# Attention's first scores ahead of the next pair's transposes, five more warm products, the first k on ScalarE's queue, and mask products in bf16 behind the others

## Chip, cores and metric

One Trainium2 chip, one core. The metric is the time of one execution in device microseconds (us). The kernel before was timed in three runs: 858.63, 860.8 and 864.05 us, a median of 860.8 us. One more execution was profiled; its rows are the ones read here.

## The reference

Three layers follow one another: block-causal attention, a mixture of experts that picks one expert per token, and a two-layer network with a leaky activation. The change touches the first alone.

```python
def _attn_ref(q, k, v):                      # q, k, v: (4, 8, 576, 64)
    scores = scale * np.matmul(q, k.transpose(0, 1, 3, 2))
    mask = block_i >= block_j                # blocks of 64 positions
    scores = np.where(mask, scores, -1000000000.0)
    scores = scores - np.max(scores, axis=-1, keepdims=True)
    attn = np.exp(scores)
    attn = attn / (np.sum(attn, axis=-1, keepdims=True) + 1e-09)
    return np.matmul(attn, v)

def reference(**kw):
    x = attn_out.transpose(0, 2, 1, 3).reshape(2304, 512)
    x = _moe_ref(x, ...)                     # gate, argmax over 8 experts, relu(x w1) w2
    return _moe2_ref(x, ...)                 # (leaky(x w_in)) w_out
```

## The kernel before

Attention runs over 16 pairs of heads (4 batches, 4 pairs each). For a pair `p`, `load` (line 186) brings q, k and v with three transfers each, all issued by SyncE's queue (SP). `tr` (line 198) transposes four 128x128 tiles of q (`psq`) or k (`psk`) on TensorE (PE); `split_qk` (line 210) has ScalarE (ACT) write the high part (`qh`, `kh`) and VectorE (DVE) the rest (`ql`, `kl`). `tr_tail` (line 218) does the same for the last 64 positions (`pst`), whose q goes into two block-diagonal tiles of `qd`.

`sc(p, i)` (line 228) makes the scores of one block of rows, in the order i = 4, 3, 2, 1, 0. For i < 4 it has n = 128 i + 128 columns of keys. Each of the three products of `PARTS` (`qh·kh`, `qh·kl`, `ql·kh`, line 236) is issued as two instructions, one for each head, on 64 rows of the array each. Between the first and the second product stands the mask product (line 239): `top` by `neg` adds -2^30 to the last 64 columns of the rows that may not see them. For i = 4 the block-diagonal `qd` needs no mask (line 243). A score block lies in one of two PSUM buffers (`ps_s`). Then `row_max` (DVE, lines 250 and 253), `expo` (ACT, lines 267 and 270), `ptr` (transposes of the exponentials on PE, lines 286 to 301, copied by ACT or DVE, lines 275 and 277), `pv` (products with v, lines 314 and 326) and `xout` (lines 350 to 358).

A table of offsets `OFF` (line 513) gives each step of each pair its place, so that the steps of neighbouring pairs interleave; a scheduler then orders the instructions of each engine by priority and its own estimates. What stands on an engine runs strictly in that order. At the start `warm` (line 57) issues eight bf16 products of 512 columns without use (`psw`), behind the first `load`, while the first transfers are under way.

After attention the tokens are routed, lists are scattered to memory and read back, and the experts run, fed by large weight loads of which two are under way at a time (`bulk`, line 78); the last layer follows.

Of the kernel before, what the change touches and what calls it, by code (L numbers as in the profile page):

```python
# [9 lines left out]
F32 = mybir.dt.float32  # L10
F32R = mybir.dt.float32r
BF16 = mybir.dt.bfloat16
I32 = mybir.dt.int32
AF = mybir.ActivationFunctionType
ALU = mybir.AluOpType
AX = mybir.AxisListType
# [3 lines left out]
B, H, S, D = 4, 8, 576, 64  # L20
# [17 lines left out]
WARM = 8  # L38
NEG = -float(2 ** 30)
# [8 lines left out]
def tile_kernel(ctx: ExitStack, tc: tile.TileContext, q, k, v, w_skip, w_gate, w1, w2, w_in, w_out, alpha, out):  # L48
    nc = tc.nc
    dram = lambda n, s, dt: nc.dram_tensor(n, s, dt, kind="Internal").ap()  # L50
    xd = dram("xd", (NT + 1, DM), F32)
    def free(ins, group):
        ins = ins.ins
        tc.declare_no_dep(ins, group=group, reason="rows of one token each")
        tc.add_to_no_dep_group(group, ins)

    def warm(pool, tag, n):
        if n == 0:
            return
        ps = pool.tile([128, 2, 4, 128], F32, tag=tag, name="psw")  # L60
        for i in range(n):
            nc.tensor.matmul(ps[:, 0], ones, ones.unsqueeze(1).to_broadcast([128, 4, 128]), start=True, stop=True)

    def apart():
        nc.gpsimd.memset(pad, 0)
# [54 lines left out]
    acst = actx.enter_context(tc.tile_pool(name="acst", bufs=1))  # L120
    ident = const.tile([128, 128], F32, name="ident")
# [5 lines left out]
    ones = const.tile([128, 128], BF16, name="ones")  # L127
# [16 lines left out]
    nc.vector.memset(fill, PADROW)  # L144
    tlo = acst.tile([128, 5], I32, name="tlo")
    nc.vector.tensor_scalar(out=tlo, in0=tok, scalar1=63, scalar2=None, op0=ALU.bitwise_and)
    top = acst.tile([128, 128], F32R, name="top")
    nc.vector.memset(top.bitcast(F32), 0.0)
    for r in (0, 64):
        nc.vector.memset(top[r:r + 1, 0:64].bitcast(F32), 1.0)  # L150
    neg = acst.tile([128, 64], F32R, name="neg")
    nc.vector.memset(neg.bitcast(F32), NEG)
    thi = acst.tile([128, 5], F32, name="thi")
    nc.vector.tensor_tensor(out=thi, in0=tok, in1=tlo, op=ALU.subtract)
    sli = const.tile([128, 2, 2], F32, name="sli")
# [23 lines left out]
    st = [dict() for _ in range(NPAIR)]  # L179
# [4 lines left out]
    half = [slice(0, 64), slice(64, 128)]  # L184

    def load(p, nm, src):
        b, h0 = p // NP, p % NP * 2
        a = ld.tile([128, 5, 2, D], F32, tag=nm + "r", name=nm + "r")
        for x in range(2):
            nc.sync.dma_start(out=a[:, 0:4, x, :], in_=src[b, h0 + x, 0:512, :].rearrange("(t p) d -> p t d", p=128))  # L190
        nc.sync.dma_start(out=a[0:64, 4], in_=src[b, h0:h0 + 2, 512:S, :].rearrange("h p d -> p h d"))
        st[p][nm + "r"] = a

    def tok4(p, nm, t):
        n = 128 if t < 4 else 64
        return st[p][nm + "r"][0:n, t].rearrange("p h d -> p (h d)")

    def tr(p, nm):
        ps = ps_m.tile([128, 512], F32, tag="m", name="ps" + nm)
        for t in range(4):  # L200
            nc.tensor.transpose(ps[:, t * 128:t * 128 + 128], tok4(p, nm, t), ident)
        for c in "hl":
            st[p][nm + c] = tp.tile([128, 512 if nm == "q" else S], F32R, tag=nm + c, name=nm + c)
        split_qk(nm, *(st[p][nm + c][:, 0:512] for c in "hl"), ps)
# [5 lines left out]
    def split_qk(nm, hi, lo, ps):  # L210
        scale = 0.125 if nm == "q" else 1.0
        nc.scalar.activation(out=hi, in_=ps, func=AF.Copy, scale=scale)
        if nm == "q":
            nc.vector.scalar_tensor_tensor(out=lo, in0=ps, scalar=scale, in1=hi.bitcast(F32), op0=ALU.mult, op1=ALU.subtract)
        else:
            nc.vector.tensor_tensor(out=lo, in0=ps, in1=hi.bitcast(F32), op=ALU.subtract)

    def tr_tail(p):
        ps = ps_m.tile([128, 2, 64], F32, tag="m", name="pst")
        for n, nm in enumerate("qk"):  # L220
            nc.tensor.transpose(ps[:, n, :], tok4(p, nm, 4), ident[0:64, 0:64])
        for x, hs in enumerate(half):
            split_qk("q", *(qd[p % 2][hs, c, x * 64:x * 64 + 64] for c in range(2)), ps[hs, 0, :])
        split_qk("k", *(st[p]["k" + c][:, 512:S] for c in "hl"), ps[:, 1, :])
# [3 lines left out]
    def sc(p, i):  # L228
        d = st[p]
        ps = d["s", i] = ps_s.tile([128, 2, 512], F32, tag="s", name="pss")  # L230
        if i < 4:
            n = 128 * i + 128
            qc = slice(i * 128, i * 128 + 128)
            for k, (a, b) in enumerate(PARTS):
                for x, hs in enumerate(half):
                    nc.tensor.matmul(ps[:, x, 0:n], d[a][hs, qc], d[b][hs, 0:n], start=(k == 0), stop=(k == 2))  # L236
                if k == 0:
                    for x, hs in enumerate(half):
                        nc.tensor.matmul(ps[:, x, n - 64:n], top[hs], neg[hs], start=False, stop=False)
        else:  # L240
            for c, o in ((slice(0, 512), ps[:, 0]), (slice(512, S), ps[:, 1, 0:64])):
                for k, (a, b) in enumerate(PARTS):
                    nc.tensor.matmul(o, qd[p % 2][:, int(a == "ql")], d[b][:, c], start=(k == 0), stop=(k == 2))

    def row_max(p, i):
        d = st[p]
        ps = d["s", i]
        if i < 4:
            m = sm.tile([128, 2], F32, tag="mx", name="mx", bufs=4)
            nc.vector.tensor_reduce(out=m, in_=ps[:, :, 0:128 * i + 128], axis=AX.X, op=ALU.max, negate=True)  # L250
        else:
            m = sm.tile([128, 1], F32, tag="m4", name="m4", bufs=2)
            nc.vector.tensor_reduce(out=m, in_=ps.rearrange("p x c -> p (x c)")[:, 0:S], axis=AX.X, op=ALU.max, negate=True)
        d["m", i] = m

    last_exp = [None]
# [262 lines left out]
    for p in range(NPAIR):  # L519
# [11 lines left out]
        if p % NP == NP - 1:  # L531
            b = p // NP
            last = p == NPAIR - 1
            n = NP - 1 if last else NP
# [25 lines left out]
    order = sorted(events)  # L560
    cut = 5 * NPAIR + OFF["xo"]
    gaps = {route2: 8, route4: 4}
    start = {load: WARM}
    for s in order:
        if s < cut:
            for fn, a in events[s]:
                fn(*a)
                warm(ps_s, "s", start.pop(fn, 0))
# [4 lines left out]
    for s in order:  # L573
        if s >= cut:
            for fn, a in events[s]:
                if fn in gaps:
                    warm(ps_s, "s", gaps[fn])
                fn(*a)
# [5 lines left out]
    ps = ps_m.tile([128, E], F32, tag="m", name="psl")  # L584
# [6 lines left out]
    def scatter(o, ids):  # L591
        free(nc.gpsimd.indirect_dma_start(out=xd, out_offset=bass.IndirectOffsetOnAxis(ap=ids, axis=0), in_=o, in_offset=None, bounds_check=NT - 1, oob_is_err=False), "xd")

    warm(ps_s, "s", 13)
    xgs = [stat.tile([128, DM], F32, tag=f"xg{g}", name="xgs") for g in range(2)]
    gather(xgs[0], sid[:, 0:1])
# [424 lines left out]
    for n, (w, f) in enumerate(seq):  # L1021
        if n + 2 < len(seq):
            g1(*seq[n + 2])
        t = (f - 5) // 2
# [43 lines left out]
```

## Time and profile before

| | |
|---|---|
| timed runs, median (lowest, highest) | 860.8 us (858.63, 864.05) |
| the profiled execution, its time | 854.09 us |
| its span, first to last instruction | 852.5 us |
| PE busy, share of the span | 799.0 us, 94% |
| DVE, ACT, GpSimd (POOL) busy | 458.8, 299.3, 162.4 us |
| mean granted clock of PE | 0.97 of full speed |
| attention's score blocks | about 12 to 241 us |

The profiled execution is 6.7 us below the median of the timed runs. A share of busy time is a mean over stages with different limits; a matmul's duration in a row contains its way through the array, so what a product costs on PE is read from the distance between the starts of rows that follow one another. "PEld" rows are the loads of the stationary operand, which can run under a product. "[idle before <-releaser]" says how long the engine stood idle and who ended that.

### The profile page before, as it was taken

How to read it: one execution, taken by the hardware profiler on the slowest of the kernel's cores; microseconds unless marked ns; L12 is line 12 of the kernel's file. 1: busy time of each engine (PE TensorE's matmuls, PEld its weight loads, DVE VectorE, ACT ScalarE, POOL GpSimd, SP SyncE). 2: the span in 40 equal slices, each digit the busy share in tenths (PEclk: the TensorE clock that was granted, in tenths of full speed). 3: DMA queues.
4: the chain of work that ended last, by engine and by line, in shares of the span. 5: the costliest groups of instructions: out<-in, count | busy, mean ns of one | idle time of the engine just before them, and what ended most of it. 6: DMA issues, size and time to landing. Idle time of an engine off the chain costs nothing.

```text
span 852.5 us, 14562 instructions
## 1 busy us (share of the span) xinstructions
PE 799.0 (94%) x5548; PEld 613.9 (72%) x5548; DVE 458.8 (54%) x951; ACT 299.3 (35%) x779; POOL 162.4 (19%) x204
## 2 busy tenths in 40 slices
PE   7999999999986899998599988999999999999998
PEld 4777777777753665765388666888888888888887
DVE  4576757667657167798579898323222332222232
ACT  3777676766641123112143433211111112111111
POOL 1000110110103122313012211321222212222132
PEclk7999999999998799999799999999999999999999
DMA  6765354464313777877723221100110001000100
GB/s 123 169 197 143 87 147 108 96 159 126 95 36 89 251 254 244 267 254 240 239 101 94 80 83 42 50 0 1 50 50 0 1 26 50 0 1 1 38 13 25
DMA packets 96378, 85.84 MB, mean 101 GB/s; under 512 B 68601, under 2 KB 73913, under 8 KB 96272
## 3 DMA queue, kind: packets, MB, share of 16 engines
q1 hardware_dynamic: 93776, 78.88, 32.1%
q0 software_dynamic: 2496, 5.61, 2.0%
q8 instruction: 59, 0.97, 0.5%
q14 instruction: 47, 0.39, 0.2%
HBM read 73.20 MB, written 11.71 MB: 100 GB/s over the span
## 4 chain that ended last, share of the span: by engine, by line
PE 47%; DVE 9%; DMA 4%; issue 2%; ACT 1%; SPq 0%; DVEq 0%; ACTq 0%
PE psf L970 18%; PE psa L1001 6%; PE psa L1002 6%; PE psa L1011 6%; PE psh L752 4%; PE psy L763 3%; DVE dt L640 2%; DMA w2t<-in_moe_w_dram 1%; DVE dr L644 1%; DVE dt L641 1%; DVE gt L983 1%; DMA w1t<-in_moe_w_dram 1%; PE psh L777 1%; DVE dr L642 1%; DVE dr L638 1%
## 5 line engine op out<-in xcount | busy, mean ns | idle before, releaser
L970 PE MATMUL psf<-xs,whi 128*128 128x512 f32 (+1 forms) x640 | 159.6, 371 | 0.7 <-ACT xs L856 0.7
L987 POOL TENSOR_TENSOR gl<-gt,gh 128x512 fp32r<-128x512 f32 (+1 forms) x80 | 96.0, 1200 | 322.9 <-ACT gh L986 190.5
L986 ACT ACTIVATE gh<-gt 128x512 fp32r<-128x512 f32 (+1 forms) x80 | 47.1, 589 | 264.5 <-PE psa L1002 144.7
L970 PEld LDWEIGHTS psf<-xs,whi 128*128 128x128 f32 x640 | 114.3, 188 | 25.4 <-ACT xs L856 0.9
L982 DVE TENSOR_SCALAR gu<-psf,alf 128x512 f32<-128x512 f32 (+1 forms) x64 | 43.7, 683 | 158.3 <-PE psf L970 158.0
L970 PE MATMUL psf<-xs,wlo 128*128 128x512 f32 (+1 forms) x320 | 80.1, 372 | 0.0
L267 ACT ACTIVATE pe<-pss,mx 128x512 f32<-128x512 f32 (+3 forms) x128 | 66.6, 524 | 14.2 <-DVE mx L250 11.8
L970 PEld LDWEIGHTS psf<-xs,wlo 128*128 128x128 f32 x320 | 56.6, 188 | 11.7
L1001 PE MATMUL psa<-whi,gh 128*128 128x512 f32 x144 | 57.3, 398 | 6.5 <-ACT gh L986 6.5
L250 DVE TENSOR_REDUCE mx<-pss 128x2 f32<-128x1024 f32 (+1 forms) x64 | 52.4, 819 | 19.9 <-PE pss L236 17.3
L275 ACT ACTIVATE pt<-pspt 128x512 f32<-128x512 f32 (+3 forms) x112 | 52.1, 488 | 29.4 <-PE pspt L301 28.7
L1001 PE MATMUL psa<-wkg,gh 128*128 128x512 f32 x144 | 57.2, 397 | 1.7 <-ACT gh L986 1.7
L983 DVE SCALAR_TENSOR_TENSOR gt<-psf,gu 128x512 f32<-128x512 f32 (+1 forms) x80 | 51.0, 637 | 13.9 <-POOL gl L987 8.1
L1002 PE MATMUL psa<-wlo,gh 128*128 128x512 f32 x144 | 56.3, 391 | 0.0
L1002 PE MATMUL psa<-wkg,gh 128*128 128x512 f32 x144 | 56.3, 391 | 0.0
L301 PE MATMUL pspt<-ident,pe 128*128 128x128 f32 x320 | 51.5, 287 | 0.1
L326 PE MATMUL pso<-pt,vr 128*64 128x256 f32 (+1 forms) x384 | 47.5, 352 | 2.3 <-ACT pt L275 2.1
L857 DVE TENSOR_TENSOR xs<-psx,xs 128x512 fp32r<-128x512 f32 x18 | 12.4, 692 | 60.4 <-ACT xs L856 60.4
L326 PEld LDWEIGHTS pso<-pt,vr 128*64 128x64 f32 x384 | 30.1, 136 | 16.9 <-ACT pt L275 7.2
L752 PEld LDWEIGHTS psh<-xT,w1t 128*128 128x128 f32 x320 | 39.5, 205 | 1.5 <-issue 1.0
L752 PE MATMUL psh<-xT,w1t 128*128 128x128 f32 x320 | 40.2, 290 | 0.0
L301 PEld LDWEIGHTS pspt<-ident,pe 128*128 128x128 f32 x320 | 33.8, 141 | 6.7 <-issue 2.2
(231 smaller groups left out, 1374.3 us busy)
## 6 DMA issues: line engine op xcount, KB each, us to landing
w1t<-in_moe_w_dram SPq DMA_DIRECT2D x32, 512.0 KB, 4.5
w2t<-in_moe_w_dram SPq DMA_DIRECT2D x32, 512.0 KB, 4.5
dr<-in_moe_w_in_dram SPq DMA_DIRECT2D x16, 512.0 KB, 5.1
dr<-in_moe_w_out_dram SPq DMA_DIRECT2D x16, 512.0 KB, 3.7
out_dram<-ob SPq DMA_DIRECT2D x18, 256.0 KB, 2.0
qr<-in_q_dram SPq DMA_DIRECT2D x32, 128.0 KB, 4.9
kr<-in_k_dram SPq DMA_DIRECT2D x32, 128.0 KB, 2.6
vr<-in_v_dram SPq DMA_DIRECT2D x32, 128.0 KB, 2.5
```

What stands on the lines that cost most here:

```text
L250: nc.vector.tensor_reduce(out=m, in_=ps[:, :, 0:128 * i + 128], axis=AX.X, op=ALU.max, negate=True)
L267: ins = nc.scalar.activation(out=pt[:, x, 0:n], in_=ps[:, x, 0:n], func=AF.Exp, bias=m[:, x:x + 1], scale=1.0, accum_out=d["sum"][:, x * 4 ...
L275: nc.scalar.activation(out=o, in_=a, func=AF.Copy)
L301: nc.tensor.transpose(ps[:, y, j, :], e[:, x, j * 128:j * 128 + 128], ident)
L326: nc.tensor.matmul(d["o"][hs, c0:c0 + n * 128], v5[:, j, x, :], pt[:, x, 2 * j:2 * j + n].rearrange("p n c -> p (n c)"), start=(j == 0), s ...
L752: nc.tensor.matmul(ps[:, f], w[:, kk, c:c + 128], self.xT[:, kk], start=(kk == 0), stop=(kk == 3))
L970: nc.tensor.matmul(ps[:, 0:n], wsp[f // 4 * 4 + kk][a][:, ws], c[:, kk, 0:n], start=(n0 == 0 and kk == 0), stop=(n0 == 2 and kk == 3))
L983: nc.vector.scalar_tensor_tensor(out=t[:, 0:n], in0=ps[:, 0:n], scalar=0.0, in1=u[:, 0:n], op0=ALU.max, op1=ALU.add)
L987: nc.gpsimd.tensor_tensor(out=lo[:, 0:n], in0=t[:, 0:n], in1=hi[:, 0:n].bitcast(F32), op=ALU.subtract)
L1001: nc.tensor.matmul(o, hi[:, ts], whi, start=(f == 0), stop=False)
L1002: nc.tensor.matmul(o, hi[:, ts], wlo, start=False, stop=False)
L1011: nc.tensor.matmul(acc[w, t], lo[:, t * 128:t * 128 + 128], whi, start=False, stop=False)
```

## The change

It makes four edits. The first three act on the first pair, the fourth on every pair.

1. The first transpose of the second pair's q waits for the first row maximum (a dependency on DVE's reduce of `sc(0, 4)`), so that the first scores stand ahead of it.
2. `warm` issues five more products behind `tr_tail` of the first pair (the first of them is kept behind the tail transposes in the schedule).
3. The three transfers of the first pair's k are issued by ACT's queue instead of SP's.
4. `top` and `neg` are bf16 and not fp32r, and the mask product stands behind the third product of `PARTS` and closes the accumulation, which the third product did before.

```diff
     def warm(pool, tag, n):
...
         for i in range(n):
-            nc.tensor.matmul(ps[:, 0], ones, ones.unsqueeze(1).to_broadcast([128, 4, 128]), start=True, stop=True)
+            ins = nc.tensor.matmul(ps[:, 0], ones, ones.unsqueeze(1).to_broadcast([128, 4, 128]), start=True, stop=True)
+            if i == 0 and tail[0]:
+                tc.add_manual_dep(ins.ins, tail[0].name, mybir.DependencyInfo(mybir.DependencyClass.NoSync, mybir.DependencyReason.SCHED_ONLY), reason="behind the transposes")
...
-    top = acst.tile([128, 128], F32R, name="top")
-    nc.vector.memset(top.bitcast(F32), 0.0)
+    top = acst.tile([128, 128], BF16, name="top")
+    nc.vector.memset(top, 0.0)
...
-    neg = acst.tile([128, 64], F32R, name="neg")
-    nc.vector.memset(neg.bitcast(F32), NEG)
+    neg = acst.tile([128, 64], BF16, name="neg")
+    nc.vector.memset(neg, NEG)
...
     def load(p, nm, src):
+        queue = nc.scalar if p == 0 and nm == "k" else nc.sync
         for x in range(2):
-            nc.sync.dma_start(out=a[:, 0:4, x, :], in_=src[b, h0 + x, 0:512, :].rearrange("(t p) d -> p t d", p=128))
+            queue.dma_start(out=a[:, 0:4, x, :], in_=src[b, h0 + x, 0:512, :].rearrange("(t p) d -> p t d", p=128))
...
     def tr(p, nm):
         for t in range(4):
-            nc.tensor.transpose(ps[:, t * 128:t * 128 + 128], tok4(p, nm, t), ident)
+            ins = nc.tensor.transpose(ps[:, t * 128:t * 128 + 128], tok4(p, nm, t), ident)
+            if p == 1 and nm == "q" and t == 0:
+                tc.add_manual_dep(ins.ins, st[0]["first"].name, mybir.DependencyInfo(mybir.DependencyClass.Sync, mybir.DependencyReason.DATA), reason="first scores first")
...
             for k, (a, b) in enumerate(PARTS):
                 for x, hs in enumerate(half):
-                    nc.tensor.matmul(ps[:, x, 0:n], d[a][hs, qc], d[b][hs, 0:n], start=(k == 0), stop=(k == 2))
-                if k == 0:
-                    for x, hs in enumerate(half):
-                        nc.tensor.matmul(ps[:, x, n - 64:n], top[hs], neg[hs], start=False, stop=False)
+                    nc.tensor.matmul(ps[:, x, 0:n], d[a][hs, qc], d[b][hs, 0:n], start=(k == 0), stop=False)
+            for x, hs in enumerate(half):
+                nc.tensor.matmul(ps[:, x, n - 64:n], top[hs], neg[hs], start=False, stop=True)
...
-    start = {load: WARM}
+    start = {load: WARM, tr_tail: 5}
```

PE at the start, before: behind the first pair's transposes of k (`psk`) and of the tails (`pst`) stand the second pair's of q (`psq`), then the first scores (`pss`).

```order
L201 MATMUL psk<-ident,kr 128x128 x4
L221 MATMUL pst<-ident,qr 128x64
L221 MATMUL pst<-ident,kr 128x64
L201 MATMUL psq<-ident,qr 128x128 x4
L243 MATMUL pss<-kh,qd_168 128x512
L243 MATMUL pss<-kl,qd_168 128x512
L236 MATMUL pss<-kh,qh 128x512 x2
L243 MATMUL pss<-kh,qd_168 128x512
```

The same place after the change (the pair of rows with `ones` stands five times).

```order
L206 MATMUL psk<-ident,kr 128x128 x4
L228 MATMUL pst<-ident,qr 128x64
L228 MATMUL pst<-ident,kr 128x64
L64 LDWEIGHTS ones
L64 MATMUL psw<-ones 128x512
...
L249 MATMUL pss<-kh,qd_168 128x512
L249 MATMUL pss<-kl,qd_168 128x512
...
L243 MATMUL pss<-kh,qh 128x512 x2
L243 MATMUL pss<-kl,qh 128x512 x2
L243 MATMUL pss<-kh,ql 128x512 x2
...
L206 MATMUL psq<-ident,qr 128x128 x4
```

The second pair's four transposes moved from ahead of the first two score blocks to behind them, and the five products `psw` stand where they were.

ACT at the start, before: the two writes of `qd` that the first scores need stand on either side of the second pair's `qh`.

```order
L212 ACT_TABLE_LOAD
L212 ACTIVATE qh<-psq 128x512
L212 ACTIVATE kh<-psk 128x512
L212 ACTIVATE qd_168<-pst 64x64
L212 ACTIVATE qh<-psq 128x512
L212 ACTIVATE qd_168<-pst 64x64
L212 ACTIVATE kh<-pst 128x64
L270 ACTIVATE p_261,sum<-pss,m_254 128x576
```

After the change:

```order
L195 DMA kr<-in_k_dram 128x4x64 x2
L196 DMA kr<-in_k_dram 64x2x64
L219 ACT_TABLE_LOAD
L219 ACTIVATE qh<-psq 128x512
L219 ACTIVATE kh<-psk 128x512
L219 ACTIVATE qd_168<-pst 64x64 x2
L219 ACTIVATE kh<-pst 128x64
L276 ACTIVATE p_267,sum<-pss,m_260 128x576
L219 ACTIVATE qh<-psq 128x512
```

Three issues of the first k came to the head of ACT's queue, and the second pair's `qh` went behind the first exponentials (`p`).

PE in the second pair, one score block of 384 columns, before (`psx` belongs to the pair ahead):

```order
L236 MATMUL pss<-kh,qh 128x384 x2
L239 MATMUL pss<-neg,top 128x64 x2
L236 MATMUL pss<-kl,qh 128x384 x2
L236 MATMUL pss<-kh,ql 128x384 x2
L350 MATMUL psx<-ident,xt 128x128 x4
```

After the change:

```order
L243 MATMUL pss<-kh,qh 128x384 x2
L243 MATMUL pss<-kl,qh 128x384 x2
L243 MATMUL pss<-kh,ql 128x384 x2
L245 LDWEIGHTS top
L245 MATMUL pss<-neg,top 128x64
L245 LDWEIGHTS top
L245 MATMUL pss<-neg,top 128x64
L356 MATMUL psx<-ident,xt 128x128 x4
```

The mask product went from between the first and second product to the end of its block, and its weight load became an instruction of its own.

## Rows read from the trace of the kernel before

**Rows 1.** Windows of the start (busy us and instructions by engine, granted clock, DMA)

```profile
core 0: us, PE busy (x) PEld busy (x) DVE busy (x) ACT busy (x) POOL busy (x), PEclk, DMA share, GB/s
7.00:9.60 2.60, 0.01 (x1) 0.00 (x0) 0.88 (x3) 0.48 (x2) 0.18 (x1) 0.94 0.65 146
11.70:22.90 11.20, 10.80 (x54) 7.23 (x55) 5.16 (x8) 4.04 (x12) 0.17 (x1) 0.50 0.74 134
22.90:28.20 5.30, 5.30 (x50) 4.42 (x49) 1.60 (x5) 4.50 (x16) 0.00 (x0) 1.00 0.99 222
```

**Rows 2.** Timeline of PE and ACT, 0 to 13 us (start us, us, engine, line)

```profile
0.94 1.28 ACT L212 ACT_TABLE_LOAD   x1 [0.94 <-PEq L1053]
...
1.26 3.59 PE L62 MATMUL psw<-ones 128*128 128x512 bf16 x8 [1.26 <-DVE ones L128]
...
4.65 1.06 PE L201 MATMUL psq<-ident,qr 128*128 128x128 f32 x4
...
6.12 0.63 PE L201 MATMUL psk<-ident,kr 128*128 128x128 f32 x4 [0.41 <-DMA kr<-in_k_dram]
...
7.28 0.20 ACT L212 ACTIVATE qd<-pst 64x64 fp32r<-64x64 f32 x1
...
9.64 1.09 PE L201 MATMUL psq<-ident,qr 128*128 128x128 f32 x4 [2.62 <-DMA qr<-in_q_dram]
...
11.75 0.77 PE L243 MATMUL pss<-kh,qd 128*128 128x512 f32 x1 [1.02 <-ACT qd L212]
```

**Rows 3.** SP's issues of the first pair's k, same columns

```profile
2.77 1.14 SPq L190 DMA_DIRECT2D kr<-in_k_dram  x2
...
3.95 0.62 SPq L191 DMA_DIRECT2D kr<-in_k_dram  x1
```

**Rows 4.** PE timeline: first score products of the second, fourth and fifth pair

```profile
28.24 0.48 PE L243 MATMUL pss<-kh,qd 128*128 128x512 f32 x1
...
55.49 0.47 PE L243 MATMUL pss<-kh,qd 128*128 128x512 f32 x1
...
69.11 0.48 PE L243 MATMUL pss<-kh,qd 128*128 128x512 f32 x1
69.42 0.39 PE L243 MATMUL pss<-kl,qd 128*128 128x512 f32 x1
69.66 0.42 PE L243 MATMUL pss<-kh,qd 128*128 128x512 f32 x2
```

**Rows 5.** PE timeline of the fifth pair, its block of 512 columns and what follows

```profile
70.14 0.44 PE L301 MATMUL pspt<-ident,pe 128*128 128x128 f32 x2
70.50 0.49 PE L236 MATMUL pss<-kh,qh 64*128 64x512 f32 x2
70.84 0.19 PE L239 MATMUL pss<-neg,top 64*128 64x64 f32 x2
70.87 0.47 PE L236 MATMUL pss<-kl,qh 64*128 64x512 f32 x2
71.18 0.40 PE L236 MATMUL pss<-kh,ql 64*128 64x512 f32 x2
71.51 0.66 PE L201 MATMUL psq<-ident,qr 128*128 128x128 f32 x4
72.09 0.87 PE L326 MATMUL pso<-pt,vr 128*64 128x256 f32 x8
72.89 0.66 PE L286 MATMUL pspt<-ident,p 128*128 128x128 f32 x4
...
74.43 0.66 PE L350 MATMUL psx<-ident,xt 128*128 128x128 f32 x4
...
75.03 0.60 PE L201 MATMUL psk<-ident,kr 128*128 128x128 f32 x4
```

**Rows 6.** Waits, 20 to 340 us: engine, line <- releaser: us, times, longest

```profile
PEld pso L326 <- ACT pt L275: 7.2, 26, 1.0
```

**Rows 7.** SP's own waits, 240 to 420 us, same columns

```profile
SPq L79 <- DMA w2t<-in_moe_w_dram: 46.2, 24, 3.9
SPq L79 <- DMA w1t<-in_moe_w_dram: 40.1, 20, 3.4
```

More of the change, by code (lines that the diff above doesn't have):

```diff
@@ L55, in free @@
         tc.add_to_no_dep_group(group, ins)
+    tail = [None]
     def warm(pool, tag, n):
@@ L146, in tile_kernel @@
     nc.vector.tensor_scalar(out=tlo, in0=tok, scalar1=63, scalar2=None, op0=ALU.bitwise_and)
-    top = acst.tile([128, 128], F32R, name="top")
-    nc.vector.memset(top.bitcast(F32), 0.0)
+    top = acst.tile([128, 128], BF16, name="top")
+    nc.vector.memset(top, 0.0)
     for r in (0, 64):
-        nc.vector.memset(top[r:r + 1, 0:64].bitcast(F32), 1.0)
-    neg = acst.tile([128, 64], F32R, name="neg")
-    nc.vector.memset(neg.bitcast(F32), NEG)
+        nc.vector.memset(top[r:r + 1, 0:64], 1.0)
+    neg = acst.tile([128, 64], BF16, name="neg")
+    nc.vector.memset(neg, NEG)
     thi = acst.tile([128, 5], F32, name="thi")
@@ L188, in load @@
         a = ld.tile([128, 5, 2, D], F32, tag=nm + "r", name=nm + "r")
+        queue = nc.scalar if p == 0 and nm == "k" else nc.sync
         for x in range(2):
-            nc.sync.dma_start(out=a[:, 0:4, x, :], in_=src[b, h0 + x, 0:512, :].rearrange("(t p) d -> p t d", p=128))
-        nc.sync.dma_start(out=a[0:64, 4], in_=src[b, h0:h0 + 2, 512:S, :].rearrange("h p d -> p h d"))
+            queue.dma_start(out=a[:, 0:4, x, :], in_=src[b, h0 + x, 0:512, :].rearrange("(t p) d -> p t d", p=128))
+        queue.dma_start(out=a[0:64, 4], in_=src[b, h0:h0 + 2, 512:S, :].rearrange("h p d -> p h d"))
         st[p][nm + "r"] = a
@@ L220, in tr_tail @@
         for n, nm in enumerate("qk"):
-            nc.tensor.transpose(ps[:, n, :], tok4(p, nm, 4), ident[0:64, 0:64])
+            tail[0] = nc.tensor.transpose(ps[:, n, :], tok4(p, nm, 4), ident[0:64, 0:64]).ins
         for x, hs in enumerate(half):
@@ L252, in row_max @@
             m = sm.tile([128, 1], F32, tag="m4", name="m4", bufs=2)
-            nc.vector.tensor_reduce(out=m, in_=ps.rearrange("p x c -> p (x c)")[:, 0:S], axis=AX.X, op=ALU.max, negate=True)
+            d["first"] = nc.vector.tensor_reduce(out=m, in_=ps.rearrange("p x c -> p (x c)")[:, 0:S], axis=AX.X, op=ALU.max, negate=True).ins
         d["m", i] = m
```

## The prediction, made before the change was run

> **What bounds the kernel now.** I read the windows of the start first, then the timeline of its first 13 us, then the timeline of a middle pair, and last the waits.
>
> The windows show a start at half clock. PE does nothing between 7.0 and 9.6 us, the granted clock falls at the end of that stretch, and it stays at 0.50 from 11.7 to 22.9 us although PE is busy 10.80 of those 11.20 us; from 22.9 us it is 1.00 [rows 1]. Those are the two levels, 1.2 and 2.4 GHz. The column says 1.00 for the first microseconds too, but four transposes took 1.06 us at 4.65 and 0.63 us at 6.12 [rows 2]: the clock was low until it rose in between, and no change had been recorded before. So the eight warm products raise the clock, and the idle stretch loses it again.
>
> The timeline says why PE is idle. The second pair's q transposes stand ahead of the first scores and wait 2.62 us for their transfer; behind them ACT writes the second pair's `qh` before the second half of `qd`, for which the first score product waits another 1.02 us, until 11.75 us [rows 2]. The first half of `qd` was begun at 7.28 us.
>
> From 28.24 us, where the second pair's scores start, PE works without gaps: a pair without routing takes 69.11 - 55.49 = 13.62 us [rows 4]. In such a pair what counts is the distance between the starts of PE's rows. Behind attention the weight loads bound the experts: SP waits 46.2 and 40.1 us in all for the loads of which two may be under way [rows 7]. That chain starts from attention's lists, so an earlier end of attention moves it whole, and nothing there takes the gain back.
>
> **Part 1: first scores first.** The first scores then need both halves of `qd`. ACT began the first at 7.28 us for 0.20 us [rows 2]; the second follows it at once, so about 7.7 us. The first score product starts about 11.75 - 7.7 = 4.05 us earlier. The second pair's q has landed by 9.64 us and is now wanted about 2 us behind the first score product, at about 9.7 us, so the moved transposes hardly wait. They now stand behind DVE's first maximum, and PE's queue behind them holds the first pair's own exponentials, which need that maximum as well: the added wait holds up nothing that was free before.
>
> **Part 2: five more products.** At the high clock a product of 512 columns costs 0.24 us (69.42 to 69.66 [rows 4]), at the low one 3.59 / 8 = 0.45 us with the tail [rows 2]: 1.2 to 2.2 us from about 6.8 us on, in a stretch that is empty. At the high clock they end at about 8.0 us, at the low one at 9.0 us, so 0.3 to 1.3 us of them can show. I take the first scores at 7.9 us; k may come earlier (part 3), which takes the 0.3 us back, hence 7.7. What they buy is the clock: with them and the scores PE goes from 6.1 us on with little idle, and the windows show a fall only behind a stretch with 0.01 us of work in 2.60 [rows 1].
>
> The first pair took 28.24 - 11.75 = 16.49 us [rows 2, 4], 11.2 of them at half clock. At the high clock it is bounded from above by the middle pair, 13.62 us, and from below by that pair less what it does for its neighbour ahead: two transposes 70.14 to 70.50 (0.36), eight products with v 72.09 to 72.89 (0.80) and the transposes of the output 74.43 to 75.03 (0.60) [rows 5], so 13.62 - 1.76 = 11.9 us. In the first pair nothing of a neighbour covers the first softmax; I add 0.3 us and take 12.2. The second pair's scores start at 7.7 + 12.2 = 19.9 us, 8.3 us earlier than before; the bounds are 9.0 + 13.6 = 22.6 (5.6 us earlier) and 7.5 + 11.9 = 19.4 (8.8 us).
>
> **Part 3: k by ACT.** SP issued the first k from 2.77 to 4.57 us [rows 3], behind q; from ACT it goes out beside q. PE waited 0.41 us for it [rows 2], and that is all it can give; q and k sharing the engines at a DMA share of 0.65 to 0.74 [rows 1] can cost q about as much, so 0.4 either way, already within part 2's bounds. The three issues, about 1.8 us, push ACT's table load (1.28 us [rows 2]) from 0.94 to about 2.7 us, done at 4.0, while the first transposes start at 4.65: hidden. SP's later transfers go out 1.8 us sooner, and no wait in the middle pairs hangs on them: nothing.
>
> **Part 4: the mask product.** In a block of 512 columns PE's steps are: first product 0.34, mask 0.03, second 0.31, third and the way to the next stage 0.33, in all 71.51 - 70.50 = 1.01 us [rows 5]. The mask itself costs 0.03. But the second product's step is 0.31 where a product whose weights were loaded under the one ahead takes 0.24 (rows 4, 69.42 to 69.66; the first there, with its load in the open, takes 0.31 too). Weights for one product ahead can be loaded; with the mask between, that one is the mask's, and the second product's come too late. With the mask last: 0.34 + 0.24 + 0.24 + 0.03, and the way out 0.33 - 0.24 = 0.09, in all 0.94, or 0.07 us less. A load of 128 columns is the same in the blocks of 384 and 256, so 0.07 each. The block of 128 columns stands ahead of products with v that wait for ACT's copies (7.2 us in 26 waits [rows 6]), which takes its gain: 0. Three blocks in 15 pairs: 45 x 0.07 = 3.1 us. The bounds are 0, if the loads stay in the open, and 60 x 0.1 = 6 us.
>
> One rule speaks against this. The Trainium skill, "TensorE: Matmul & The Clock Gate", section "Part 3: Packing small matmuls — row/col tiling", says that a weight load overlaps a running matmul only when the two use different row groups, and the second product uses the rows of the first. By that rule part 4 gives nothing. The step of 0.24 us against 0.31 for two products on all rows [rows 4] does not agree with it; on half of the rows no row shows it.
>
> DVE's smaller fills of `top` and `neg`, and single instructions that the scheduler exchanged in the pairs with routing, are the same work in another place: nothing, at most 1 us either way.
>
> **The sum.** 8.3 + 3.1 = 11.4 us. The profiled execution took 854.09 us, 852.5 of span and 1.6 around it, so 842.7 us. The median of the timed runs is 860.8, 6.7 us above the profiled one; I take the same distance: 849.4 us.
>
> **Rivals.**
> A. The clock does not stay up. For it: from 11.7 to 22.9 us PE was busy 96% of the time and the clock did not rise [rows 1]; much of the first pair is transposes. Then the five products cost 2.2 us, the first scores stand at 9.0 us, and the first pair is at least as long as before, 16.5 us, more likely 18 since its last 5.3 us were at the high clock: the second pair starts at 27.0, a gain of 1.2. With part 4, 860.8 - 4.3 = 856.5 us. Against it: the idle stretch ahead of the fall is gone. The Trainium skill, "TensorE: Matmul & The Clock Gate", section "Part 4: PE-mode transpose", states that transposes on PE don't count as busy for the clock. That would make this rival likelier; no row here tells the two kinds of work apart.
> B. The weight loads stay in the open on half of the rows: the step of 0.24 us is from products on all rows [rows 4], and on half rows the second product's step is 0.31 [rows 5], which would then stay. Part 4 gives 0: 860.8 - 8.3 = 852.5 us. Against it: the third product's step is no longer than the 0.33 that a hidden load and the way out need. The rule of the Trainium skill in part 4 is this rival's.
> C. The mask products cost instead. If bf16 between fp32r products empties the array, each block pays another way out, 0.09 us, and its two weight loads, now instructions of their own, in the open, at about 0.11 us each (four transposes, each with its load, and the switch behind them take 0.58 us from 71.51 on, a fifth of that is 0.12 [rows 5]): 0.31 - 0.07 = 0.24 us for each of 64 blocks, 15.4 us, less 8.3: 867.9 us. It turns the change slower from 8.3 / 64 = 0.13 us a block on. Against it: the mask stays on the same half rows as its neighbours.
> D. The order does what it says, but the first pair is bound by ACT and DVE and takes the full 13.6 us, with the products ending late: the gain is 5.6 + 3.1 = 8.7, so 852.1 us, the upper end of my forecast.
>
> **How the numbers follow.** The forecast (with D inside it) has 0.65, its own range 845 to 854; A 0.17, B 0.12, C 0.06. A measurement of this kernel can tell about 1% from no change, that is 8.6 us. Below 852.2 us lie 0.8 of the forecast (0.52), half of B (0.06) and a little of A (0.03): 0.61. Above 869.4 lies part of C: 0.03. The rest, 0.36, is within 1%. The range of 844 to 858 us takes in A and B and leaves out C and tails of about 0.1.
>
> **What would show it.** Right: the first score product before 8.5 us, a granted clock of 1.00 from about 7 us to the end of attention, the second pair's first score near 20 us, middle pairs of 13.4 us, and in a block of 512 columns two steps of 0.24 and a mask step of 0.1 to 0.15. Wrong: a stretch at 0.50 between 8 and 23 us (A), a second step of 0.31 (B), a mask step of 0.3 or more, or middle pairs over 13.62 us (C). The forecast falls altogether if the second pair starts as early as I say and the end doesn't move: then something behind attention is not tied to it.

## The result, and the profile after

The changed kernel took 849.1 us in the median of four runs (846.28 to 853.85), the kernel before, timed beside it, 860.6 us (858.63 to 864.05): a ratio of 0.9894, with a 95% interval of 0.9855 to 0.9934. The forecast was 849.4. The profiled execution took 847.79 us, with a span of 846.2. The page has PE busy for 788.9 us (93%), DVE for 459.3 and ACT for 297.9 us.

The windows of the start, in the columns of [rows 1], come first. The last row is the third pair behind the first, a middle pair (one that has no routing work around it).

```profile
7.00:9.60 2.60, 2.06 (x14) 1.46 (x12) 1.48 (x5) 0.44 (x2) 0.00 (x0) 1.00 0.63 142
10.40:20.00 9.60, 9.23 (x91) 6.65 (x91) 6.16 (x15) 8.02 (x29) 0.17 (x1) 1.00 0.71 125
...
46.96:60.52 13.56, 13.20 (x126) 10.00 (x124) 8.47 (x20) 10.04 (x31) 0.17 (x1) 1.00 0.74 185
```

From 7.0 to 9.6 us PE is now busy 2.06 of 2.60 us, where it did 0.01 us of work before, and the granted clock is 1.00 in every row: the stretch at 0.50 from 11.7 to 22.9 us [rows 1] is gone.

The timeline of the start shows why; it answers to [rows 2, 3].

```profile
0.94 1.09 ACTq L195 DMA_DIRECT2D kr<-in_k_dram  x2
2.79 1.28 ACT L219 ACT_TABLE_LOAD   x1 [2.79 <-issue]
...
5.19 0.60 PE L206 MATMUL psk<-ident,kr 128*128 128x128 f32 x4
...
5.98 1.25 PE L64 MATMUL psw<-ones 128*128 128x512 bf16 x5
...
7.78 0.47 PE L249 MATMUL pss<-kh,qd 128*128 128x512 f32 x1 [0.54 <-issue]
...
9.85 0.65 PE L206 MATMUL psq<-ident,qr 128*128 128x128 f32 x4
...
19.82 0.48 PE L249 MATMUL pss<-kh,qd 128*128 128x512 f32 x1
...
219.63 0.48 PE L249 MATMUL pss<-kh,qd 128*128 128x512 f32 x1
```

ACT issues k and loads its table behind it, from 2.79 to 4.07 us, ahead of the transposes, as forecast. The k transposes start at 5.19 us and not at 6.12. The five products fill PE to 7.23 us, and the first score product starts at 7.78 us (before 11.75). The second pair's q transposes stand behind the first scores, at 9.85 us, and wait for nothing. The second pair's scores start at 19.82 us (before 28.24): 8.42 us earlier, forecast 8.3.

By the last pair the gain is 229.83 - 219.63 = 10.20 us (229.83 is the start of that row before). So the middle of attention gave 1.78 us more, where part 4 promised 3.1. A middle pair tells why. Here are its PE rows, the one load that waits, and DVE's rows; they answer to [rows 4, 5].

```profile
46.96 0.48 PE L249 MATMUL pss<-kh,qd 128*128 128x512 f32 x1
...
48.35 0.50 PE L243 MATMUL pss<-kh,qh 64*128 64x512 f32 x2
48.69 0.39 PE L243 MATMUL pss<-kl,qh 64*128 64x512 f32 x2
48.92 0.40 PE L243 MATMUL pss<-kh,ql 64*128 64x512 f32 x2
49.16 0.20 PE L245 MATMUL pss<-neg,top 64*128 64x64 bf16 x2
49.29 0.66 PE L206 MATMUL psq<-ident,qr 128*128 128x128 f32 x4
49.40 1.22 DVE L256 TENSOR_REDUCE mx<-pss 128x2 f32<-128x1024 f32 x1 [0.46 <-PE pss L245]
50.66 0.69 DVE L221 SCALAR_TENSOR_TENSOR ql<-psq,qh 128x512 fp32r<-128x512 f32 x1
51.27 0.68 DVE L283 COPY xt<-pso 128x512 f32<-128x512 f32 x1
51.86 0.68 DVE L283 COPY pt<-pspt 128x512 f32<-128x512 f32 x1
52.46 0.95 DVE L256 TENSOR_REDUCE mx<-pss 128x2 f32<-128x768 f32 x1
53.33 0.68 DVE L363 TENSOR_TENSOR xr<-psx,rb 128x512 f32<-128x512 f32 x1
...
53.27 0.38 PE L243 MATMUL pss<-kh,qh 64*128 64x256 f32 x2
...
53.73 0.20 PE L245 MATMUL pss<-neg,top 64*128 64x64 bf16 x2
54.06 0.81 PEld L320 LDWEIGHTS pso<-pt,vr 128*64 128x64 f32 x20 [0.24 <-DVE xr L363]
...
60.52 0.48 PE L249 MATMUL pss<-kh,qd 128*128 128x512 f32 x1
```

In the block of 512 columns the distances between starts are 0.34, 0.23, 0.24 and, from the mask to the next stage, 0.13 us: 0.94 in all, 0.07 less than the 1.01 of [rows 5], as worked out. The rows of the weight loads of the second product (`kl` by `qh`), first of before, then of after, show what changed:

```profile
70.84 0.19 PEld L236 LDWEIGHTS pss<-kl,qh 64*128 64x128 f32 x2
```

```profile
48.46 0.19 PEld L243 LDWEIGHTS pss<-kl,qh 64*128 64x128 f32 x2
```

Before, this load began when the mask product ran, 0.03 us ahead of its own product (70.87 [rows 5]); now it lies under the first product, which runs from 48.35 us on.

But the pair takes 60.52 - 46.96 = 13.56 us where 13.4 was forecast. PE stands still ahead of the product with v of the last 64 rows (line 320, `pso4`) until DVE's multiply `xr` ends at 53.33 + 0.68 = 54.01 us. That multiply empties the PSUM buffer of the outputs' transposes (`psx`), and `pso4` is the next tile of the pool `ps_m` to use it. DVE has no gap from 49.40 us on: one maximum, one split, two copies, another maximum, then the multiply.

The waits of the 28th to the 230th us, ahead of that product, first of before (a row not shown ahead of the prediction), then of after, in the columns of [rows 6]:

```profile
PEld pso L314 <- DVE xr L357: 2.6, 14, 0.2
```

```profile
PEld pso L320 <- DVE xr L363: 1.9, 8, 0.2
```

By this view the wait for `xr` was already there, and even larger. The experiments show that most of what it lists there before was not a wait that cost anything.

SP's waits for the experts' weights, 240 to 420 us, stand at 49.1 and 37.7 us in all, against 46.2 and 40.1 [rows 7]: nothing new behind attention.

```profile
SPq L83 <- DMA w2t<-in_moe_w_dram: 49.1, 24, 4.5
SPq L83 <- DMA w1t<-in_moe_w_dram: 37.7, 18, 3.0
```

### The profile page after: what moved, and what is told of

It reads as the page before. It is cut to its first block, busy times and chain, and to the rows that moved or that the text cites. A ratio compares the mean times of both kernels' runs of the same rounds, so it can differ in the third digit from the quotient of the medians.

```text
span 846.2 us, 14578 instructions
## 1 busy us (share of the span) xinstructions
PE 788.9 (93%) x5553; PEld 606.3 (72%) x5553; DVE 459.3 (54%) x951; ACT 297.9 (35%) x779; POOL 162.8 (19%) x204
## 4 chain that ended last, share of the span: by engine, by line
PE 38%; DVE 9%; issue 2%; DMA 1%; ACT 1%; DVEq 0%; SPq 0%; ACTq 0%
PE psf L976 18%; PE psa L1007 6%; PE psa L1008 6%; PE psa L1017 6%; DVE dt L646 2%; DVE dr L650 1%; DVE dt L647 1%; DVE gt L989 1%; DVE dr L648 1%; DVE dr L644 1%; DVE wkg L634 1%; DVE dt L645 1%; DVE dt L643 1%; PE psx L964 1%; DMA out_dram<-ob 1%
## 5 line engine op out<-in xcount | busy, mean ns | idle before, releaser
L989 DVE SCALAR_TENSOR_TENSOR gt<-psf,gu 128x512 f32<-128x512 f32 (+1 forms) x80 | 51.0, 637 | 14.2 <-POOL gl L993 8.4
L643 DVE TENSOR_SCALAR dt<-dr 128x512 int32<-128x512 int32 x29 | 17.0, 587 | 41.0 <-DMA dr<-in_moe_w_in_dram 36.6
L1017 PE MATMUL psa<-wkg,gl 128*128 128x512 f32 x140 | 38.4, 392 | 0.0
```

Source lines behind the costliest of these rows:

```text
L989: nc.vector.scalar_tensor_tensor(out=t[:, 0:n], in0=ps[:, 0:n], scalar=0.0, in1=u[:, 0:n], op0=ALU.max, op1=ALU.add)
L1017: nc.tensor.matmul(acc[w, t], lo[:, t * 128:t * 128 + 128], whi, start=False, stop=False)
```

## The experiments

The eleven runs in one table. The ratio is to the kernel before on the same chip, with its 95% interval. The other columns are the starts of a pair's first score product (line 249) and the distance between two of them, in us, from the timeline of each profiled execution. The ratio's interval is 2 to 5.5 us to either side, so the profile's starts, of one execution each, decide between the theories, and the ratio says whether they arrive at the end.

| kernel | ratio | first pair's scores | second pair's | a middle pair | last pair's |
|---|---|---|---|---|---|
| before | 1 | 11.75 | 28.24 | 13.63 | 229.83 |
| changed | 0.9894 (0.9855 to 0.9934) | 7.78 | 19.82 | 13.57 | 219.63 |
| changed, again | 0.9883 (0.9843 to 0.9923) | 8.38 | 20.43 | 13.57 | 220.26 |
| mask change alone | 0.9983 (0.9958 to 1.0008) | 11.88 | 28.12 | 13.57 | 227.99 |
| without the mask change | 0.9915 (0.9882 to 0.9948) | 8.21 | 19.79 | 13.63 | 222.28 |
| without the five products | 0.9921 (0.9889 to 0.9954) | 7.84 | 21.15 | 13.57 | 221.00 |
| without the order | 0.9958 (0.9928 to 0.9987) | 9.78 | 23.91 | 13.57 | 223.84 |
| first k by SP | 0.9897 (0.9833 to 0.9961) | 8.73 | 20.79 | 13.57 | 220.83 |
| mask last, in fp32r | 0.9880 (0.9821 to 0.9940) | 8.69 | 20.20 | 13.55 | 220.54 |
| `pso4` freed | 0.9853 (0.9812 to 0.9893) | 8.45 | 20.98 | 13.37 | 217.65 |
| `pso4` freed, again | 0.9878 (0.9830 to 0.9926) | 7.69 | 20.21 | 13.37 | 216.84 |
| `pso4` freed, mask as before | 0.9883 (0.9847 to 0.9919) | 8.25 | 20.96 | 13.58 | 220.71 |
| `pso4` freed, a copy by DVE | 0.9823 (0.9775 to 0.9871) | 7.90 | 20.01 | 12.99 | 214.64 |

### The mask change alone, and everything but it

The first is the kernel before with edit 4, the second the changed kernel with edit 4 undone:

```diff
-                    nc.tensor.matmul(ps[:, x, 0:n], d[a][hs, qc], d[b][hs, 0:n], start=(k == 0), stop=False)
-            for x, hs in enumerate(half):
-                nc.tensor.matmul(ps[:, x, n - 64:n], top[hs], neg[hs], start=False, stop=True)
+                    nc.tensor.matmul(ps[:, x, 0:n], d[a][hs, qc], d[b][hs, 0:n], start=(k == 0), stop=(k == 2))
+                if k == 0:
+                    for x, hs in enumerate(half):
+                        nc.tensor.matmul(ps[:, x, n - 64:n], top[hs], neg[hs], start=False, stop=False)
```

Expected of the mask change alone:

> The kernel before with the mask products last and in bf16, nothing else of the change. Theory (the products take less, but TensorE then waits for the score tile of the last 64 rows' product, whose PSUM buffer VectorE's multiply by the reciprocals releases): the block of 512 takes 0.94 us from its first product to the next work (before 1.01), a middle pair 13.57 us (before 13.63), the first pair some 16.4 us, the whole 1.5 to 2 us less than before. The prediction's sum: a middle pair of 13.42 us, 3.1 us less than before. Third (bf16 products between fp32r ones cost): a block of 512 at 1.01 or more, and no gain.

Expected without it:

> The changed kernel with the mask products as before (in fp32r, second of four). Theory: the second pair's first score product stands at 20.0 us (with the whole change 19.8), the clock is 1.00 from 4.8 us on, a middle pair takes 13.63 us, the whole 8.4 us less than before. Rival (the start needs the mask change as well): the second pair's scores at 20.5 us or later.

Alone, the mask change makes a middle pair 13.57 us and the last pair's scores 229.83 - 227.99 = 1.84 us earlier, as the theory said and not the 3.1 us of the prediction. In the timed runs that is a ratio of 0.9983, whose interval reaches 1. Without the mask change the second pair's scores stand at 19.79 us and a middle pair takes 13.63 us; the last pair's scores come 229.83 - 222.28 = 7.55 us earlier, and the ratio is 0.9915. The two shares add up to 9.39 of the 10.20 us. Of the missing 0.81 us, 0.56 is the place of the first score product, which stood at 11.88 and 8.21 us in these two runs and moves by some tenths from run to run (below). The place of the second pair's scores alone misleads in the second run: its first pair took 11.58 us, but its second 14.53, because PE waits there, at 23.16 us, 0.91 us for the third pair's q from DMA. With the mask last in fp32r (below) the same wait is 0.42 us, in the changed kernel's two profiles there is none.

### The buffer of `pso4` freed, with the mask change and without

To take the suspected wait away, `pso4` gets its PSUM buffer from the pool of the other outputs (`ps_o`), which is empty at that time. Its step and that of the transposes behind it move in the offset table, so that the scheduler keeps TensorE's order in the middle pairs as it was; around the routing the order differs.

```diff
-            ps = ps_m.tile([128, 64], F32, tag="m", name="pso4")
+            ps = ps_o.tile([128, 64], F32, tag="o", name="pso4")
...
-                at(s0 + n + OFF[u], fn, p, i)
+                at(s0 + {("V", 4): 3.1, ("T", 3): 3.15}.get((u, i), n + OFF[u]), fn, p, i)
```

Expected:

> The changed kernel with the output tile of the last 64 query rows in the PSUM pool of the other outputs, so that its buffer no longer comes free with VectorE's multiply of the outputs. The order of TensorE's work in the middle pairs stays as in the changed kernel. Theory: the wait of 0.23 us ahead of that product goes, a middle pair takes 13.34 us (changed kernel 13.57), the whole 3 us less than the changed kernel. Rival (ScalarE's copies of the transposed weights hold the pair anyway): TensorE waits 0.2 us longer ahead of the products with v of the other rows, a middle pair stays at 13.57, the whole stays.

The same with the mask products as before:

> As the run with the freed output tile, but with the mask products as before (fp32r, second of four). Theory: with that wait out of the way the mask change is worth its full size, so a middle pair takes 13.54 us here against 13.34 with the masks last in bf16: 0.2 us a pair, 3 us in all. Rival (ScalarE's copies hold the pair): both take the same, 13.57.

The block of 256 columns and the product behind it, with the mask change (the same block as at 53.27 us above):

```profile
54.02 0.38 PE L243 MATMUL pss<-kh,qh 64*128 64x256 f32 x2
...
54.48 0.20 PE L245 MATMUL pss<-neg,top 64*128 64x64 bf16 x2
54.61 0.95 PE L320 MATMUL pso<-pt,vr 128*64 128x64 f32 x20
```

The same place with the masks as before:

```profile
54.59 0.39 PE L243 MATMUL pss<-kh,qh 64*128 64x256 f32 x2
...
55.24 0.95 PE L321 MATMUL pso<-pt,vr 128*64 128x64 f32 x20
```

From the block's first product to the product with v it is now 54.61 - 54.02 = 0.59 us with the mask change, against 54.06 - 53.27 = 0.79 in the changed kernel and 55.24 - 54.59 = 0.65 with the masks as before. No wait for `xr` is left. The middle pairs take 13.37 and 13.58 us: with the wait gone, the mask change is worth 0.21 us a pair, three blocks of 0.07, which is the prediction's own figure. So the steps of part 4 were right, and in a middle pair the wait for DVE took two thirds of their sum. TensorE's, DVE's and ACT's orders in a middle pair are those of the kernels with the buffer shared, so the buffer alone makes this difference there.

The four middle pairs together show a chain of two limits. With the masks as before, freeing the buffer gives 13.63 - 13.58 = 0.05 us; with the masks last, it gives 13.57 - 13.37 = 0.20. Before the change PE came to this product almost when DVE let it go: from the start of the block of 256 to the product with v it took 0.65 us with the buffer free, and 49.03 - 48.32 = 0.71 in the kernel before, whose rows for it are these:

```profile
48.32 0.39 PE L236 MATMUL pss<-kh,qh 64*128 64x256 f32 x2
...
49.03 0.95 PE L314 MATMUL pso<-pt,vr 128*64 128x64 f32 x20
```

The waits view put that wait at 2.6 / 14 = 0.19 us each, but only 0.06 of it held PE up; the other 0.13 us pass there with the buffer free as well.

Timed, the freed tile gave ratios of 0.9853 and, in the run below, 0.9878.

### Without the five products

```diff
-    start = {load: WARM, tr_tail: 5}
+    start = {load: WARM}
```

> The changed kernel without the five warm products. Theory (they hold the clock over ScalarE's and VectorE's share of the first pair): TensorE has nothing from 5.9 to 7.7 us, the granted clock falls to 0.50 within the first pair, which takes 14 to 16.5 us instead of 12.0; the second pair's scores start at 22 to 24 us, the whole is 2 to 4 us longer than the changed kernel. Rival (the order alone brings it, and the first scores keep the clock by themselves): 1.00 throughout, the second pair's scores at 19.8 us, the same time.

PE's timeline, the first score product:

```profile
7.84 0.47 PE L249 MATMUL pss<-kh,qd 128*128 128x512 f32 x1 [1.77 <-ACT qd L219]
```

Windows of the first pair, from 8.2 us to the second pair's scores, in the columns of [rows 1]:

```profile
8.20:11.60 3.40, 3.40 (x16) 2.45 (x15) 1.29 (x3) 0.84 (x3) 0.00 (x0) 0.51 0.70 155
11.70:21.10 9.40, 9.11 (x91) 6.55 (x90) 5.97 (x15) 7.83 (x27) 0.17 (x1) 1.00 0.75 136
```

The clock does fall, behind the 1.77 us in which PE waits for `qd`, and it is back after some 3.4 us. The first pair takes 13.31 us where 14 to 16.5 was expected (12.04 in the changed kernel). So the second pair's scores stand at 21.15 us, 1.33 later than in the changed kernel, and not at 22 to 24. The mechanism is the theory's; the price is a third to two thirds of what I gave it, because the clock comes back much sooner than it did before the change (22.9 us [rows 1]).

### Without the order

The dependency of the second pair's q transposes on the first maximum is left out:

```diff
-            if p == 1 and nm == "q" and t == 0:
-                tc.add_manual_dep(ins.ins, st[0]["first"].name, mybir.DependencyInfo(mybir.DependencyClass.Sync, mybir.DependencyReason.DATA), reason="first scores first")
```

> The changed kernel without the dependency that puts the second pair's transposes behind the first maximum; the five products stay. TensorE's four transposes then stand ahead of the first score product again, and ScalarE's copy of them between the two halves of the first pair's other operand. Theory: with k by ScalarE's queue the second q comes earlier than it did before, so the price is smaller than the 4 us that I gave to the order: first score product at 9 to 11 us, the clock kept or lost with the length of the gap that is left; the second pair's scores at 21 to 23 us if it is kept, 26 if not. Rival (the order is worth nothing once the clock is held): 19.8 us.

The timeline of PE and ACT around the first scores:

```profile
8.13 0.63 PE L206 MATMUL psq<-ident,qr 128*128 128x128 f32 x4 [0.98 <-DMA qr<-in_q_dram]
8.79 0.60 ACT L219 ACTIVATE qh<-psq 128x512 fp32r<-128x512 f32 x1 [2.32 <-PE psq L206]
9.41 0.22 ACT L219 ACTIVATE qd<-pst 64x64 fp32r<-64x64 f32 x1
9.78 0.47 PE L249 MATMUL pss<-kh,qd 128*128 128x512 f32 x1 [1.02 <-ACT qd L219]
```

Both waits of [rows 2] are back: 0.98 us for the second q (before 2.62, since SP issues q at 4.61 us instead of 6.45, now that k is on another queue) and 1.02 us for the half of `qd` behind ACT's copy, as before. The first scores start 2.00 us later and the second pair's 4.09 us later (23.91), a little over the range of 21 to 23. The clock stays at 1.00 over the gap and the first scores (9.78 to 14.20 us), and is 0.82 on average from 14.2 to 23.9 us: it stands at 0.50 from 14.7 to 18.1 us. So the 4.09 us hold a loss of clock as well, which the run doesn't tell apart from the waits. Undoing the order costs three times what undoing the five products does.

### The first k on SP's queue

```diff
-        queue = nc.scalar if p == 0 and nm == "k" else nc.sync
+        queue = nc.sync
```

> The changed kernel with the first k on SyncE's queue. Theory: the transposes of k start at 6.1 us as before the change instead of 5.2, so everything up to the second pair's scores is some 0.9 us later: first score product at 8.6 us, second pair's scores at 20.7 us. The prediction: 0.4 us either way. Rival (the start is bound by ScalarE's table load and copies): first scores at 7.8 us as with the change.

PE's timeline of the start:

```profile
4.65 1.06 PE L206 MATMUL psq<-ident,qr 128*128 128x128 f32 x4
6.16 0.74 PE L206 MATMUL psk<-ident,kr 128*128 128x128 f32 x4 [0.45 <-DMA kr<-in_k_dram]
...
8.73 0.47 PE L249 MATMUL pss<-kh,qd 128*128 128x512 f32 x1 [0.38 <-issue]
```

The k transposes go back to 6.16 us, the first scores to 8.73 and the second pair's to 20.79: 0.97 us later than in the changed kernel's first profile, as the theory said. But that profile was among the luckiest. In the nine profiles with k by ACT and the first scores first, the first score product stood between 7.69 and 8.69 us, at 8.21 in the middle one (the table's third column). Two things move it. In four of the nine PE first waits 0.32 to 0.43 us for q (the transposes of q began at 4.63 to 5.19 us, where with k by SP they began at 4.65 in each of the three); that q and k share the way in would explain it, but no run shows that. And the first change to a granted clock of 1.00 that the traces record stands between 4.0 and 7.0 us: where it stands behind 6 us the four transposes of q took 1.08 to 1.09 us, elsewhere 0.63 to 0.70. In the run shown here it came at 6.4 us, in the changed kernel's first profile at 4.8, so part of the 0.97 us is the clock's. Beside the changed kernel's second profile, where it came at 6.3 us, the edit is worth 8.73 - 8.38 = 0.35 us, and beside the middle one of the nine 8.73 - 8.21 = 0.5.

### The mask last, but in fp32r

The place of the change with the type of before, so that the two are told apart:

```diff
-    top = acst.tile([128, 128], BF16, name="top")
+    top = acst.tile([128, 128], F32R, name="top")
...
-    neg = acst.tile([128, 64], BF16, name="neg")
+    neg = acst.tile([128, 64], F32R, name="neg")
```

> The changed kernel with the mask products last, as in the change, but in fp32r. Theory (the place makes the gain, since the second product's weights can then be loaded under the first; the type gives nothing or little): second step of a block of 512 at 0.23 to 0.24 us as in bf16, the mask's own step at most 0.05 longer, middle pair 13.57 us. Rival (the type makes it): the mask's step is 0.1 us or more longer than in bf16 and a middle pair goes back to 13.63 us or over.

PE's timeline of a block of 512 columns in a middle pair:

```profile
49.11 0.50 PE L243 MATMUL pss<-kh,qh 64*128 64x512 f32 x2
49.45 0.39 PE L243 MATMUL pss<-kl,qh 64*128 64x512 f32 x2
49.68 0.40 PE L243 MATMUL pss<-kh,ql 64*128 64x512 f32 x2
49.91 0.19 PE L245 MATMUL pss<-neg,top 64*128 64x64 f32 x2
50.03 0.66 PE L206 MATMUL psq<-ident,qr 128*128 128x128 f32 x4
```

The second step is 0.23 us as in bf16, the mask's step 0.12 (bf16 0.13), a block of 512 takes 0.92 (0.94) and a middle pair 13.55. The place made the gain; the type gave nothing.

### A copy by DVE, with `pso4` freed

With the wait for `xr` gone, the largest one left in a pair is that for ACT's copies of the transposed exponentials, ahead of the products with v. On the kernel with `pso4` freed, one of the two copies of the block of 384 columns goes to DVE; PE's order stays the same. Two more kernels ran beside it, the changed one and the freed one again.

```diff
-ON_ACT = ("0", "1", "2a", "2b", "3a", "3b", "5", "xt")
+ON_ACT = ("0", "1", "2a", "3a", "3b", "5", "xt")
```

> The changed kernel itself, so that it stands on the same chip as the two versions beside it. From its first timing: 0.989 of the kernel before, last pair's scores at 219.6 us.

> The run with the freed output tile once more, beside the changed kernel. Theory: 15 times 0.20 us less than the changed kernel (13.37 against 13.57 us a middle pair), so 3 us or 0.0035 below it in the ratio to the kernel before; by the first timing of both it was 0.004. Rival (the difference of the first timing was the chip's): the same ratio within 0.001.

> The freed output tile, and one of the two copies of the transposed weights of the block of 384 columns, for which TensorE waits ahead of the products with v, made by VectorE instead of ScalarE; TensorE's order is the same. Theory (with the wait for VectorE's multiply gone, this is the wait that ends last): TensorE waits up to 0.4 us less there, a middle pair 13.0 to 13.2 us instead of 13.37, the whole 3 to 5 us less. Rival (the maximum of the last block comes later behind the copy on VectorE, and with it the exponentials): a middle pair at 13.37 us or more.

Its timeline, from one pair's first score product to the next one's:

```profile
46.00 0.48 PE L249 MATMUL pss<-kh,qd 128*128 128x512 f32 x1
...
56.20 0.56 DVE L283 COPY pt<-pspt 128x384 f32<-128x384 f32 x1 [0.30 <-PE pspt L307]
56.37 0.49 ACT L281 ACTIVATE pt<-pspt 128x384 f32<-128x384 f32 x1
56.91 0.41 PEld L332 LDWEIGHTS pso<-pt,vr 128*64 128x64 f32 x6 [0.33 <-ACT pt L281]
...
58.99 0.48 PE L249 MATMUL pss<-kh,qd 128*128 128x512 f32 x1
```

The two copies now run side by side, and a middle pair takes 58.99 - 46.00 = 12.99 us, the low end of what was expected. The last pair's scores start at 214.64 us, 5.62 earlier than in the changed kernel beside it (220.26), and 2.20 earlier than with the freed tile alone (216.84). The medians stand in the same order, 843.0, 847.1 and 849.5 us, ratios of 0.9823, 0.9878 and 0.9883 to before, but the intervals overlap.

For the freed tile alone the two timings disagree in size: 0.9853 the first time, 0.9878 now, beside a changed kernel at 0.9883. Its profile said the same both times: 13.37 us a pair, and from the second pair's scores to the last pair's 216.84 - 20.21 = 196.63 us, against 220.26 - 20.43 = 199.83. So it saves 3.2 us within attention by the profiles. By the marks set ahead of the run the second timing sides with the rival, since the two ratios differ by 0.0005; with intervals ten times as wide to either side, the timed runs are too coarse to confirm or refute the 3.2 us.

## Why the prediction was right, and where it was not

The time came out at 849.1 us for a forecast of 849.4, and the forecast case was the one that happened. That the two agree to 0.3 us is luck. Attention's last scores came 10.20 us earlier, not the 11.4 of the sum, and 9.57 in the changed kernel's second profile. The medians differ by 860.59 - 849.14 = 11.45 us with an interval of 5.7 to 12.5, and by 9.6 us the second time. Step by step:

- **The bottleneck of the start** was named rightly. The waits that the order removes come back, one of them at the same 1.02 us, when the order is undone, and the clock falls when the five products go.
- **Part 1**: first score product at 7.7 us; measured 7.78, in later profiles up to 8.69.
- **Part 2**: first pair 12.2 us, measured 12.04; gain at the second pair 8.3, measured 8.42. The total was right, but the text gave the shortening of the pair to the five products ("what they buy is the clock"). Undone one at a time, the order costs 4.09 us and the products 1.33. Together with k's 0.35 to 0.97 that is 5.8 to 6.4 of 8.42, so 2 us or more show only where several are missing: with none of the edits the clock was low from 11.7 to 22.9 us at least, and without the products alone for some 3.4 us.
- **Part 3**: 0.4 us "either way". It is 0.35 to 0.5 beside comparable profiles, on the good side, within a spread of 1 us by when q lands and when the clock rises.
- **Part 4** is the step that failed. Its steps are right to the hundredth: 0.94 us a block, 0.07 less, and 0.21 us a pair once nothing else is in the way. But the sum took all 45 blocks' gains to the end, on the ground that "PE works without gaps". It measured 1.78 us in the changed kernel from the second pair's scores on, and 1.84 alone with the first pair in it, and not 3.1. DVE, 62% busy in such a pair (8.47 of 13.56 us), works without a gap from the maximum of the block of 512 to the multiply `xr` that PE then waits for, 4.6 us before and after (44.37 to 48.97, 49.40 to 54.01). Only what the first block saves, 0.07 us, moves the start of that chain and so the end of the wait; what the blocks of 384 and 256 save ends in it. Of the 14 distances between the second and the last pair's scores, eight are middle pairs, which gave 8 x 0.065 = 0.5 us; the other six lie around a routing in twos, and each two gave 30.85 - 30.43 = 0.42 us (15.69 + 15.16 before, 12.77 + 17.66 after), so 1.3 in all. That is as much as 2 x 0.21, but the order of the work around the routing changed too, and no run here separates the two.
- **The distance to the median**, 6.7 us, was taken over from one profiled execution. That one had ended 622.7 us behind its last pair's scores; the profiles here lie between 620.1 (freed tile) and 628.8 (changed, again). What lies behind attention spreads by more than part 4 is worth, and a profiled time that is low says little about the next one. The sum gives 842.7 us for the profiled execution, which took 847.79, with the median 1.35 us above it and not 6.7: two misses of some 5 us that cancel.

The rivals: **A** is refuted by the granted clock of 1.00 over the whole first pair, transposes and all. **B** is refuted by the second step on half of the rows: 0.23 us with the mask behind, in bf16 and in fp32r. The rule of the Trainium skill, "TensorE: Matmul & The Clock Gate", section "Part 3: Packing small matmuls — row/col tiling", that a weight load overlaps a running matmul only on other row groups, does not hold for these rows: the load at 48.46 us lies within the first product's row (48.35 to 48.85), whose two instructions use both halves of the rows. **C** is refuted by the mask's step of 0.13 us, way out included, where it needed 0.24 more than before. **D** is refuted by 12.04 us against 13.6.

## What to carry to other kernels

A gain on the busiest engine is worth only as much as it moves the next wait: follow it to the first instruction that waits for another engine, and ask where that engine's own unbroken chain begins, since only what is saved ahead of that point goes through. A buffer that rotates through a shared pool is such a wait without a data dependency, and another pool can remove it. Test edits one at a time and together: here two edits of the start were worth 1.3 and 4.1 us by their removal, and two of the middle 0.05 and 0.06 us alone but 0.26 together.

## What the runs showed of the hardware

- A mask product of 64 columns on half of the rows costs the same behind the others in bf16 and in fp32r (0.13 and 0.12 us to the next stage). Between two products it looked cheaper, 0.03 us, but made the next step 0.31 instead of 0.23 us. I expected this from the steps of [rows 4, 5]; that the type plays no part I had not.
- After 1.77 us without work PE ran its first 0.4 us at the high clock, then 3.4 us at the low one, and was back at 1.00 with the transposes of the second pair. Before the change the low stretch lasted 11.2 us and more with PE busy 96% of it [rows 1]. No run here tells why one was so much longer than the other.
- A wait in the waits view can hold time that stays when its cause is gone: 0.19 us was listed ahead of `pso4`, and freeing the buffer gave 0.05 to 0.06.
- The first recorded change to a granted clock of 1.00 came between 4.0 and 7.0 us in thirteen profiles that all began with the same eight products, and the four transposes of the first q took 0.63 to 1.09 us with it.
